# Chunk 0 of a delta-rule attention: U by 32-token blocks in the first half, step sizes in G's rows and x's diagonal, unread products between all stages, chunk 1's queries sooner

## The chip, the cores and the metric

The kernel runs on one core of a Trainium2 chip. The core has a matrix engine (PE, with its weight loads listed as PEld), a vector engine (DVE), an activation engine (ACT), a general engine (POOL) and a queue engine that issues most DMAs (SP). Each engine runs its instructions in order and waits on semaphores for the others. The metric is the device time of one execution in microseconds. The median of three runs of the kernel before is 638.62 us (637.84 to 638.83).

## The reference

Two things are computed, one after the other. First comes a linear attention with the delta rule, for 4 batches, 8 heads, 768 tokens and head dimension 48:

```python
k_n = k / (norm(k) + 1e-6)
state = zeros((B, H, D, D))
for t in range(S):
    kt, vt, bt = k_n[:, :, t], v[:, :, t], beta[:, :, t, None]
    y[:, :, t] = einsum('bhd,bhde->bhe', q[:, :, t], state)
    v_old = einsum('bhde,bhd->bhe', state, kt)
    state = state + bt * einsum('bhd,bhe->bhde', kt, vt - v_old)
```

Then a feed-forward layer over the 3072 tokens of 384 features that come out: `h = x @ w_in` (2048 wide), `g = h * sigmoid(h)`, `out = g @ w_out`. Weights arrive as 64-bit floats and are narrowed to 32 bits in the kernel.

## The kernel before, in words

**Chunks and halves.** The 768 tokens are cut into six chunks of 128, each into two halves of 64. Within a half, the recurrence becomes algebra: with A the scores of keys against later keys, the updates U of all tokens solve a triangular system whose inverse XI is built explicitly, and U is XI applied to v less what the state already holds. U (called z, tile `zbuf`) then gives the outputs (`first_outputs`, `new`) and the state's update (`update`). Batches go in two groups g (batches 0 and 1, batches 2 and 3). The two heads of a pair lie in opposite halves of the 128 partitions.

**The inverse of chunk 0.** `first_score` makes A on PE; `block_out` and `block_in` send its 32x32 diagonal blocks through DRAM, so that each of the 128 partitions holds one block as tile g, and x starts as the identity (`block_room`). `norm_steps` gets the key lengths on DVE, and `block_steps` the step size of every token (tile step). `invert_first` inverts the two 16x16 corners of all blocks on DVE: it scales g by step (L668), adds 15 rank-one updates (L676, L680), scales x by step (L683), and transposes x twice (L690, L694). PE, which has nothing to do meanwhile, runs unread products (`busy`, L347, 384 columns) so timed that some wait for steps 0, 1, 2, 4, 8 and 15, and the transposes of chunk 1's keys behind steps 10, 12, 14 and 15 (`turn`, L500).

**From corners to 64x64.** `joins(0)` then runs ten stages on PE, each for one group and each followed by copies on ACT and DVE: `corner` (L717, DVE L724) completes the 32x32 blocks, `turned` (L733) and `straight` (L746) give the 32x32 inverses in both orientations, and `merge_half` (L806), twice per group, gives the block that joins two 32-token blocks. Four `masks` on DVE (L1364) zero the query scores at and below the diagonal. `inner` (L840) multiplies the 64x64 inverse with v, `first_outputs` (L884) makes the outputs, and DVE's L893 completes their transposed form xT. From there the hidden layer (`hidden`, L1046) starts, into which a written text of letters (`script`) then weaves all further work of chunk 0's second half and chunk 1: r is one half of a hidden block, f a step of narrowing weights, j one product of `joins(1)`, q the transposes of one batch of chunk 1's queries, s a step of `solve`, b the start of a narrowing.

**Order.** `pin` ties every compute instruction behind the one before it on its engine, so the order in the program is the order on each engine. `in_line` does the same for SP's DMAs. The entries of `loads` are DMAs that are issued when a count of PE's instructions (4 for a product, 2 for a transpose) reaches a number. Narrowing a piece of weights takes two ACT instructions (L233, L234), two on DVE (L238, L242) and one on POOL (L246). PSUM has eight banks in three sets: A and CC, three each, and M, two, which the transposes of chunk 1 and the hidden layer use.

Of the kernel before, what the change touches and what calls it, by code (L numbers as in the profile page):

```python
# [19 lines left out]
def kernel(  # L20
# [322 lines left out]
    def busy(n=1, after=None, how=NoSync, wide=DM):  # L343

        for _ in range(n):
            pw = bank(CC, "pw")
            done = pin(nc.tensor.matmul(  # L347
                pw[:, 0:wide], lhsT=ident[:],
                rhs=states[0][:].rearrange("p u a w -> p (u a w)")[:, 0:wide], start=True, stop=True,
            ))  # L350
# [203 lines left out]
    def block_room(c):  # L554
# [10 lines left out]
        pin(nc.gpsimd.memset(x[:, 0 : T * T : T + 1], 1.0))  # L565
# [97 lines left out]
    def invert_first(step):  # L663
# [19 lines left out]
        yield pin(nc.vector.tensor_tensor(  # L683
            out=x2, in0=x2, in1=of.unsqueeze(3).to_broadcast([P, 2, Q, Q]), op=ALU.mult
        ))
# [55 lines left out]
        def straight(g, hf):  # L741
# [9 lines left out]
            for odd in (1, 0):  # L751
# [83 lines left out]
    def inner(c, g, hf, room=CC):  # L835

        pz = bank(room, "pz")
# [7 lines left out]
        if c == 0 and hf == 0:  # L845
            by = (by_act, by_dve) if g == 0 else (by_dve, by_act)
            at = slab[:, g * HB * NP * 2 * D + D :][:, 0 : HB * NP * 2 * D]
            by[0](at.rearrange("p (n w) -> p n w", w=2 * D)[:, :, 0:D], pz[:, 0:DM].rearrange("p (n d) -> p n d", d=D))
            by[1](to, by_heads(pz))
        else:  # L850
            by_act(to, by_heads(pz))
# [126 lines left out]
    def solve(c):  # L978

        if c == 0:  # L980
            together(inner(0, 0, 0, CC))
            together(inner(0, 1, 0, M))
            yield
            first_outputs(0)
            yield
# [334 lines left out]

    for b in range(2):
# [7 lines left out]
    first_queries(1)  # L1329
    step = block_steps(0)  # L1330
    for t in xis:
# [7 lines left out]
    busy(1)  # L1339
    for b in range(2, B):  # L1340
        turn(0, b, 1, M)
    for b in range(2, B):
# [4 lines left out]
        (WINDOW + PACKET * 3 + 90, fetch_w_in, 3),  # L1347
        (WINDOW + PACKET * 4 + 15, load_q, 1, slice(HB * 0, HB * 0 + HB)),
# [6 lines left out]
        (WINDOW + PACKET * 15 + 45, fetch_w_out, 3),  # L1355
        (WINDOW + PACKET * 15 + 60, fetch_w_out, 4),
# [5 lines left out]
    def masks(g, u):  # L1362
        to = aps[0, g][1][:, u]
        pin(nc.vector.tensor_tensor(  # L1364
            out=to, in0=to, in1=above[:].unsqueeze(1).to_broadcast([P, H, W]), op=ALU.mult
        ))

    for n in range(1 + Q):
        done = next(inv)
        if n in (0, 1, 2, 4, 8):  # L1370
# [13 lines left out]
    def joins(hf, between=()):  # L1384

        for stage in (
# [4 lines left out]
            for what in between[:1]:  # L1391
                what()
            between = between[1:]

    def filled(n):
        return lambda: fill(n)

    def sized():
        size_half(0, pins[seen_on])
        begin_next()  # L1400

    def none():
        pass

    together(joins(0, [
        lambda: (size_half(0, pins[seen_on]), begin_next(),),
        lambda: (),
        lambda: (),
        lambda: (fill(1), fill(1),),
        lambda: (fill(1),),  # L1410
        lambda: (),
        lambda: (fill(1),),
        lambda: (fill(1), begin_next(),),
        lambda: (),
        lambda: (),
    ]))
    masks(0, 0)
    masks(0, 1)
    masks(1, 0)
    masks(1, 1)  # L1420

# [217 lines left out]
```

## Time and profile before

| | before |
|---|---|
| median of three runs | 638.62 us (637.84 to 638.83) |
| the profiled execution, first to last instruction | 636.1 us |
| mean granted PE clock | 0.986 |
| PE busy | 622.4 us (98%) |
| DVE busy | 397.5 us (62%) |
| ACT busy | 214.3 us (34%) |
| POOL busy | 89.9 us (14%) |

The profiled execution has no time of its own beside its span of 636.1 us; the median of the runs is 2.5 us above that span. Times in rows are microseconds from the first instruction. A row of the timeline has start, duration, engine, line, operation, output and inputs, shapes and count, and in brackets how long the engine was idle before and what ended the wait. A product of 32-bit floats shows as two records, so x6 are three products. The ends of matmuls are modelled: each record's duration includes a tail that overlaps with the next one. "issue" in the chain of waits is time in which nothing that the profile shows was waited for. In rows of stretches the number behind the busy times is the granted clock of PE, 1.00 being full and 0.50 half.

### The profile page before, as it was taken

The page shows a single profiled execution, that of the slowest core. Times are in us where ns is not written, and L with a number is a line of the kernel's source. Part 1 is how long each engine was busy: PE and PEld are TensorE (multiplying, and loading weights), DVE is VectorE, ACT ScalarE, POOL GpSimd, SP SyncE. Part 2 cuts the span into 40 slices and gives each one's busy share as a digit, 9 for nine tenths or more (in the row PEclk, how much of TensorE's full clock was granted, in tenths as well). Part 3 has the DMA queues.
Part 4 walks back from the last instruction along what each step waited for, and adds up shares of the span by engine and source line. Part 5 has one row for each costly group of instructions (what it writes and reads, how often), then busy time and mean ns, then how long its engine had stood idle before and what let it go on. Part 6 is the DMA issues. An engine that isn't in the chain of part 4 may idle for free.

```text
span 636.1 us, 21387 instructions
## 1 busy us (share of the span) xinstructions
PE 622.4 (98%) x9406; PEld 547.3 (86%) x9406; DVE 397.5 (62%) x910; ACT 214.3 (34%) x500; POOL 89.9 (14%) x92
## 2 busy tenths in 40 slices
PE   7979999999999999999999999999999999999997
PEld 5568788656799989989989989989989989989997
DVE  5786879999677974546974555975455964112112
ACT  3456673423351122451122451122451122441120
POOL 5033721345020020020020010020002000000000
PEclk9779999999999999999999999999999999999999
DMA  7966726350458460459151359232253133010101
GB/s 114 227 159 177 218 67 148 100 99 4 95 105 174 72 104 8 94 107 183 37 91 21 75 124 164 56 84 29 64 117 76 26 75 37 16 38 1 26 0 26
DMA packets 145676, 54.70 MB, mean 86 GB/s; under 512 B 117152, under 2 KB 138912, under 8 KB 145584
## 3 DMA queue, kind: packets, MB, share of 16 engines
q1 hardware_dynamic: 143136, 52.93, 40.5%
q8 instruction: 74, 1.21, 0.8%
q10 hardware_dynamic: 2448, 0.41, 0.4%
q14 instruction: 18, 0.15, 0.1%
HBM read 40.14 MB, written 11.01 MB: 80 GB/s over the span
## 4 chain that ended last, share of the span: by engine, by line
PE 94%; DVE 2%; DMA 1%; issue 1%; ACTq 0%; ACT 0%; POOL 0%; SPq 0%; DVEq 0%; POOLq 0%
PE phid L1046 40%; PE px L1163 17%; PE py L1163 13%; PE po L1090 5%; PE pb_c L840 3%; PE pa L529 2%; PE pb_c L828 2%; PE pyc L919 2%; PE pb_c L1090 2%; PE pb_c L860 2%; PE pyc L906 1%; PE px L782 1%; PE py L782 1%; PE pt L500 1%; DMA sums_of_w<-blocks 1%
## 5 line engine op out<-in xcount | busy, mean ns | idle before, releaser
L1046 PE MATMUL phid<-xT,w_in 128*128 128x256 f32 x1152 | 257.0, 381 | 0.2 <-DVE xT L893 0.2
L1046 PEld LDWEIGHTS phid<-xT,w_in 128*128 128x128 f32 x1152 | 216.4, 190 | 30.2 <-issue 0.9
L1056 ACT ACTIVATE gT<-phid 128x512 f32<-128x512 f32 x88 | 52.5, 597 | 144.8 <-PE phid L1046 140.5
L1144 DVE TENSOR_TENSOR sums_of_g<-gT 128x384 f32<-128x384 f32 (+1 forms) x60 | 30.4, 529 | 65.7 <-ACT gT L1056 55.4
L627 DVE SCALAR_TENSOR_TENSOR rank<-g,step,x 128x31 f32<-128x31 f32 (+15 forms) x124 | 49.8, 401 | 21.7 <-DMA g<-blocks 18.1
L1163 PE MATMUL px<-sums_of_w,sums_of_g 128*128 128x192 f32 x320 | 56.6, 329 | 0.0
L1163 PE MATMUL py<-w_out,sums_of_g 128*128 128x192 f32 x320 | 56.2, 328 | 0.0
L1163 PEld LDWEIGHTS py<-w_out,sums_of_g 128*128 128x128 f32 x320 | 52.3, 190 | 0.3
L1163 PEld LDWEIGHTS px<-sums_of_w,sums_of_g 128*128 128x128 f32 x320 | 52.2, 190 | 0.4
L632 DVE TENSOR_TENSOR x<-x,rank 128x31 f32<-128x31 f32 (+15 forms) x124 | 42.5, 342 | 4.3
L467 POOL TENSOR_TENSOR vf<-vf,n_slot 128x768 f32<-128x768 f32 x10 | 14.8, 1494 | 174.4 <-DMA vf<-in_v_dram 150.4
L544 ACT COPY xT<-pyc 48x128 f32<-48x128 f32 (+2 forms) x126 | 32.7, 260 | 1.7
L488 DVE STREAM_TRANSPOSE kq<-stage 128x512 f32<-128x512 f32 x28 | 28.4, 1115 | 5.2 <-DMA stage<-in_q_dram 5.2
L1163 PE MATMUL py<-w_out,gT 128*128 128x192 f32 x160 | 28.9, 330 | 0.0
L1174 DVE TENSOR_TENSOR o<-o,kept 128x192 f32<-128x192 f32 (+1 forms) x29 | 11.5, 422 | 26.7 <-ACT kept L1171 26.7
L1163 PE MATMUL px<-w_out,gT 128*128 128x192 f32 x160 | 27.9, 327 | 0.0
L1163 PE MATMUL px<-sums_of_w,gT 128*128 128x192 f32 x160 | 27.8, 327 | 0.0
L1163 PEld LDWEIGHTS px<-w_out,gT 128*128 128x128 f32 x160 | 26.5, 190 | 0.6
L550 POOL COPY g<-x 64x256 f32<-64x256 f32 x4 | 5.0, 1242 | 151.9 <-DVE x L635 151.9
L1163 PEld LDWEIGHTS py<-w_out,gT 128*128 128x128 f32 x160 | 26.1, 190 | 0.4
L865 DVE TENSOR_TENSOR state<-state,pb_c 128x384 f32<-128x384 f32 x22 | 11.2, 550 | 24.1 <-PE pb_c L860 24.1
L1163 PEld LDWEIGHTS px<-sums_of_w,gT 128*128 128x128 f32 x160 | 26.2, 190 | 0.1
(222 smaller groups left out, 931.2 us busy)
## 6 DMA issues: line engine op xcount, KB each, us to landing
vf<-in_v_dram SPq DMA_DIRECT2D x48, 96.0 KB, 2.8
out_dram<-o SPq DMA_DIRECT2D x42, 96.0 KB, 2.2
w_out<-in_moe_w_in_dram SPq DMA_DIRECT2D x4, 768.0 KB, 4.7
sums_of_w<-in_moe_w_out_dram SPq DMA_DIRECT2D x4, 768.0 KB, 4.1
blocks<-ap SPq DMA_DIRECT2D x44, 64.0 KB, 1.9
g<-blocks SPq DMA_DIRECT2D x5, 512.0 KB, 3.5
kb<-in_k_dram SPq DMA_DIRECT2D x12, 192.0 KB, 4.2
kb<-in_k_dram SPq DMA_DIRECT2D x24, 96.0 KB, 4.3
```

The lines of the kernel that those rows point to most:

```text
L467: pin(nc.gpsimd.tensor_tensor(out=vf, in0=vf, in1=of, op=ALU.mult))
L488: pin(nc.vector.transpose(out=kqs[c, b][:, :, j, :].rearrange("p a (i m) -> p a m i", i=T), in_=src.rearrange("p a (m d) -> p a m d", d=D) ...
L529: pin(nc.tensor.matmul(pa[e][half, p * n * W : (p + 1) * n * W], lhsT=kq[rows, p, 0, half], rhs=kq[rows, p, js[0] : js[-1] + 1, half], sta ...
L544: return pin(nc.scalar.copy(to, of))
L627: pin(nc.vector.scalar_tensor_tensor(out=tv, in0=g[:, 0:m, m : m + 1].to_broadcast([P, m, n]), scalar=step[:, m : m + 1], in1=x[:, m : m + ...
L632: yield pin(nc.vector.tensor_tensor(out=x[:, 0:m, m:T], in0=x[:, 0:m, m:T], in1=tv, op=ALU.add))
L840: yield pin(nc.tensor.matmul(pz[rows, n * D : (n + 1) * D], lhsT=xis[g][rows, u * H + 2 * p + e, :], rhs=vfs[c][rows, hf, g * HB + u, p, : ...
L1046: pin(nc.tensor.matmul(ph[:, j * GT : (j + 1) * GT], lhsT=w_in[:, a, (2 * f + j) * P : (2 * f + j + 1) * P], rhs=xTs[c, hf][:, a, :], star ...
L1056: pin(nc.scalar.activation(out=hidden_of(c, hf, f), in_=ph[:], func=ACTF.Silu, scale=-0.5 if in_blocks(c) else 0.5))
L1090: pin(nc.tensor.matmul(pos[i][:, 0:DM], lhsT=hidden_of(0, hf, f // 2)[:, at : at + C], rhs=w_outs[f // HFF][:, f % HFF, :], start=(f == 0) ...
L1144: pin(nc.vector.tensor_tensor(out=sums_of_g[:, k, fs], in0=of[0], in1=of[1], op=op))
L1163: pin(nc.tensor.matmul(to, lhsT=at, rhs=quarter(f, *b) if isinstance(b, tuple) else sums_of_w[b][:, f], start=start and f == 0, stop=f == ...
```

## The change: what it does

- **Step sizes.** G's rows are scaled by the step sizes, not its columns; x starts with the step sizes on its diagonal (a POOL copy behind `block_steps`) and not with ones. The scaling of x behind the inversion (L683) goes.
- **U by blocks.** In the first half, `turned`, both `merge_half` and `inner` are gone. `first_block` makes U of the first 32 tokens, `across` takes what these contribute to the last 32 tokens' right side and DVE adds it to v, and `last_block` makes U of the last 32 tokens. ACT copies U to the slab for the outputs, and DVE copies it whole to z (`keep_last`).
- **Unread products.** A product of 512 columns in the banks M (`warm`) stands behind the second `corner`, behind each of the eight stages that follow and between the two `first_outputs`. During the inversion, one waits for every even step up to 14 and one stands behind the last transpose; one more is added ahead of the second pair's queries.
- **Order.** Group 0's masks move ahead of the inversion, group 1's behind the second `across`. v is scaled before the slab is cleared. Chunk 1's queries (first half) are loaded ahead of the fourth piece of w_in; two loads of w_out have lower counts. The text begins "s s f5 q j16 q j16" instead of "s f3 s q q s j32": the transposes of two batches of chunk 1's queries stand among the corners of the second half, and two more steps of narrowing stand behind the first outputs.

```diff
-        pin(nc.gpsimd.memset(x[:, 0 : T * T : T + 1], 1.0))
+        if c > 0:
+            pin(nc.gpsimd.memset(x[:, 0 : T * T : T + 1], 1.0))
...
-            out=g2, in0=g2, in1=of.unsqueeze(2).to_broadcast([P, 2, Q, Q]), op=ALU.mult
+            out=g2, in0=g2, in1=of.unsqueeze(3).to_broadcast([P, 2, Q, Q]), op=ALU.mult
...
-        yield pin(nc.vector.tensor_tensor(
-            out=x2, in0=x2, in1=of.unsqueeze(3).to_broadcast([P, 2, Q, Q]), op=ALU.mult
-        ))
...
-            for odd in (1, 0):
+            for odd in ((0, 1) if hf == 0 else (1, 0)):
...
+    def blocks_of(k):
+        return slice(W * k, W * k + T), slice(W * k + T, W * (k + 1))
+    both_blocks = {}
+    def first_block(g):
+        pz = both_blocks[g] = bank(CC, "pz")
+        for u, p, e, n, _, _ in of_heads():
+            even, _ = blocks_of(e ^ g)
+            yield pin(nc.tensor.matmul(
+                pz[even, n * D : (n + 1) * D], lhsT=xis[g][even, u * H + 2 * p + e, 0:T],
+                rhs=vfs[0][even, 0, g * HB + u, p, :], start=True, stop=True,
+            ))
+        for k, by in enumerate((by_act, (by_dve, by_act)[g])):
+            even, _ = blocks_of(k)
+            by(zbuf[even, g * HB : (g + 1) * HB, 0, :, 0:D], by_heads(pz)[even])
+    def across(g):
+        pr = bank(A, "pr")
+        for u, p, e, n, _, _ in of_heads():
+            even, odd = blocks_of(e ^ g)
+            yield pin(nc.tensor.matmul(
+                pr[odd, n * D : (n + 1) * D], lhsT=aps[0, g][0][even, u, 2 * p + e, T:W],
+                rhs=zbuf[even, g * HB + u, 0, p, 0:D], start=True, stop=True,
+            ))
+        for k in range(2):
+            _, odd = blocks_of(k)
+            to = vfs[0][odd, 0, g * HB : (g + 1) * HB]
+            pin(nc.vector.tensor_tensor(out=to, in0=to, in1=by_heads(pr)[odd], op=ALU.add))
+    def last_block(g):
+        pz = both_blocks[g]
+        for u, p, e, n, _, _ in of_heads():
+            even, odd = blocks_of(e ^ g)
+            yield pin(nc.tensor.matmul(
+                pz[odd, n * D : (n + 1) * D], lhsT=xis[g][odd, u * H + 2 * p + e, T:W],
+                rhs=vfs[0][odd, 0, g * HB + u, p, :], start=True, stop=True,
+            ))
+        at = slab[:, g * HB * NP * 2 * D + D :][:, 0 : HB * NP * 2 * D]
+        by_act(at.rearrange("p (n w) -> p n w", w=2 * D)[:, :, 0:D], pz[:, 0:DM].rearrange("p (n d) -> p n d", d=D))
...
+    masks(0, 0)
+    masks(0, 1)
     step = block_steps(0)
+    pin(nc.gpsimd.tensor_copy(
+        out=blocks[0][2].rearrange("p s t -> p (s t)")[:, 0 : T * T : T + 1], in_=step[:]
+    ))
...
-    busy(1)
+    busy(2)
...
-        (WINDOW + PACKET * 3 + 90, fetch_w_in, 3),
-        (WINDOW + PACKET * 4 + 15, load_q, 1, slice(HB * 0, HB * 0 + HB)),
+        (WINDOW + PACKET * 3 + 90, load_q, 1, slice(HB * 0, HB * 0 + HB)),
+        (WINDOW + PACKET * 4 + 15, fetch_w_in, 3),
...
-        (WINDOW + PACKET * 15 + 45, fetch_w_out, 3),
-        (WINDOW + PACKET * 15 + 60, fetch_w_out, 4),
+        (WINDOW + PACKET * 14 + 173, fetch_w_out, 3),
+        (WINDOW + PACKET * 14 + 188, fetch_w_out, 4),
...
-    for n in range(1 + Q):
+    for n in range(Q):
         done = next(inv)
-        if n in (0, 1, 2, 4, 8):
+        if n % 2 == 0 and n < Q - 1:
             busy(1, done, Sync)
...
         if n == 15:
-            busy(1, done, Sync)
             turn(1, 3, 0, M)
+            busy(1)
     corner, turned, straight = next(inv)
+    size_half(0, pins[seen_on])
     pin(nc.gpsimd.memset(slab, 0.0))
...
-    together(joins(0, [
-        lambda: (size_half(0, pins[seen_on]), begin_next(),),
...
-    ]))
-    masks(0, 0)
-    masks(0, 1)
-    masks(1, 0)
-    masks(1, 1)
+    def keep_last(g):
+        by_dve(zbuf[:, g * HB : (g + 1) * HB, 0, :, 0:D], by_heads(both_blocks.pop(g)))
+    def warm(n=1):
+        busy(n, wide=2 * GT, room=M)
+    for stage, then in (
+        (corner(0, 0), lambda: begin_next()),
+        (corner(1, 0), lambda: (fill(2), warm())),
+        (straight(0, 0), lambda: warm()),
+        (straight(1, 0), lambda: warm()),
+        (first_block(0), lambda: (fill(1), warm())),
+        (first_block(1), lambda: (begin_next(), warm())),
+        (across(0), lambda: warm()),
+        (across(1), lambda: (masks(1, 0), masks(1, 1), warm())),
+        (last_block(0), lambda: (keep_last(0), warm())),
+        (last_block(1), lambda: (keep_last(1), warm())),
+    ):
+        together(stage)
+        then()
...
-        "s f3 s q q s j32 b j20 r f j8 ...
+        "s s f5 q j16 q j16 b j20 r f j8 ...
```

In `solve(0)`, the two calls of `inner` go and a `warm` stands between the two `first_outputs`.

More of the change, by code (lines that the diff above doesn't have):

```diff
@@ L980, in solve @@
         if c == 0:
-            together(inner(0, 0, 0, CC))
-            together(inner(0, 1, 0, M))
-            yield
             first_outputs(0)
+            warm()
             yield
@@ L1319, in first_queries, with masks @@
         score(0, b, (1,), (A, CC), evacuate)
+    def masks(g, u):
+        to = aps[0, g][1][:, u]
+        pin(nc.vector.tensor_tensor(
+            out=to, in0=to, in1=above[:].unsqueeze(1).to_broadcast([P, H, W]), op=ALU.mult
+        ))
     for b in range(2):
```

45 lines of the change are left out of this document (8 added, 37 removed).

## The prediction

> **What bounds the kernel now.** I read the busy time and clock by stretches first, then the PE waits, then the chain of waits. Stretches: us from the start, length; busy us of PE, PEld, DVE, ACT, POOL with counts; granted clock; DMA share; GB/s.
>
> ```profile
> 33.63:38.45 4.82, 3.79 (x259) 3.33 (x259) 4.34 (x8) 2.65 (x5) 2.85 (x2) 1.00 0.46 86
> 38.45:48.69 10.24, 8.20 (x275) 8.00 (x279) 8.75 (x17) 4.86 (x11) 1.83 (x1) 0.50 0.63 185
> 48.69:52.46 3.77, 3.62 (x198) 3.23 (x191) 3.03 (x6) 3.10 (x7) 1.91 (x1) 1.00 0.55 109
> 52.46:636.20 583.74, 578.92 (x8346) 513.95 (x8346) 359.13 (x805) 190.32 (x448) 73.43 (x62) 1.00 0.39 79
> ```
>
> From 52.46 us, where the first product of the hidden layer starts, PE is busy for 578.92 of 583.74 us. All its waits behind that point:
>
> ```profile
> PE pyc L919 <- issue: 0.8, 1, 0.8
> PE pb_c L828 <- ACT ap L544: 0.4, 1, 0.4
> PE phid L1046 <- DVE xT L893: 0.2, 1, 0.2
> ```
>
> They add up to 1.4 us, so a microsecond won or lost before 52.46 arrives at the end. The change lies before it. The chain of waits there (start, us, what):
>
> ```profile
> 31.52 0.99 DVE sums_of_w L683
> ...
> 33.58 1.82 DVE sums_of_w L694
> ...
> 35.61 0.36 DVE sums_of_w L724
> ...
> 38.09 1.05 issue
> ...
> 41.62 1.35 issue
> ...
> 46.71 1.60 PE pz L840 x30
> ...
> 52.33 0.14 issue
> 52.46 1.53 PE phid L1046 x6
> ```
>
> DVE's inversion leads up to 35.40, then PE leads, with holes of 1.05 and 1.35 us, at half clock from 38.45 to 48.69. The question is when the changed kernel's PE reaches that first hidden product. The profile gives a span of 636.1 us and no time of its own beyond it; the median of the runs is 638.62, so I carry 2.5 us around the span unchanged.
>
> **The change, part by part.** *Step sizes.* L683 (0.99 us) goes; scaling G by rows is the same instruction as by columns. DVE's last transpose would end at 34.38 instead of 35.40. POOL now copies 32 step sizes into x's diagonal, behind ACT's copy of the steps; its nearest row is L691, and the first user is the first rank update:
>
> ```profile
> 18.82 0.19 ACT L450 COPY step<-pg 128x32 f32<-128x32 f32 x1 [0.33 <-PE pg L445]
> 22.06 0.69 DVE L668 TENSOR_TENSOR sums_of_w<-sums_of_w,step 128x512 f32<-128x512 f32 x1 [3.01 <-DMA sums_of_w<-blocks]
> 31.33 0.63 POOL L691 COPY sums_of_w<-pick 128x512 f32<-128x512 f32 x1 [18.33 <-DVE rank L676]
> 45.32 2.50 DVE L1364 TENSOR_TENSOR ap<-ap,above 128x512 f32<-128x512 f32 x4
> ```
>
> It can end at 19.64 and is needed at 22.75: zero (0.6 at most without this cover). The two clears of xi queue behind it and are needed only near 38. *Masks.* Two of four (0.63 each) move into DVE's 3.01 us wait for the blocks, the others behind the additions of the second group: zero. They hid nothing before either: 45.32 to 47.82 lay beside L840, which ran until 48.31. *POOL order*: v is scaled before the slab is cleared; about 1.5 us each, done by 37.4, needed after 39: zero. The additions (32x384) and block copies are at most a 128x384 copy, on DVE and on ACT:
>
> ```profile
> L547 DVE COPY z<-pb_c 128x384 f32<-128x384 f32 x1 | 0.6, 557 | 0.0
> ...
> L544 ACT COPY xT<-py 128x384 f32<-128x384 f32 x2 | 1.0, 481 | 0.2 <-PE py L884 0.2
> ```
>
> Two take 1.1 us at most, and between a group's stage and its user lie two unread products and the other group's stage (3.0, below): zero. Without that cover this would be up to 1.1 us at each of five hand-overs (rival A).
>
> *PE, up to the corners.* Step 14 of the inversion ends at 31.04 and the corners start at 33.63:
>
> ```profile
> 14.97 2.20 PE L347 MATMUL pb_c<-state,ident 128*128 128x384 f32 x6
> ...
> 30.82 0.22 DVE L680 TENSOR_TENSOR sums_of_w<-sums_of_w,rank 128x56 f32<-128x56 f32 x1
> ...
> 32.29 0.60 PE L500 MATMUL pt<-ident,kb 128*128 128x128 f32 x4
> 33.63 0.20 PE L717 MATMUL pl<-sums_of_w,ap 32*32 32x16 f32 x2 [0.74 <-DVE sums_of_w L690]
> ```
>
> A matmul is two records, so x6 are three unread products of 384 columns, 0.73 each. Now eight follow even steps, and one the last transpose. Step 12 ends some 1.1 us before step 14; its product and four transposes (0.60 less 0.16 of tail that overlaps) hold PE until about 31.25. Behind that stand step 14's product, two groups of four transposes and one more product: 31.25 + 0.75 + 0.88 + 0.75 gives 33.6, and I take 33.7 with the entries. So PE itself is late and the 1.02 us of DVE buys nothing: first loss.
>
> *Stages.* PE's busy time in five short stretches, each of one line: L717 (128 records, two corners), L733 (32 records, 32 columns, two blocks of the array in turn), L746 (64, four blocks), L884 (48) and L840 (64 at half clock):
>
> ```profile
> 33.50:35.30 1.80, 1.59 (x128) 1.43 (x128) 1.00 0.55 103
> 54.80:55.53 0.73, 0.68 (x32) 0.60 (x32) 1.00 0.67 255
> 57.30:58.23 0.93, 0.87 (x64) 0.76 (x64) 1.00 0.94 344
> 50.20:51.20 1.00, 0.93 (x48) 0.79 (x48) 1.00 0.94 186
> 44.70:48.50 3.80, 3.65 (x64) 3.49 (x64) 0.50 0.55 104
> ```
>
> Each has 0.19 of tail under which the next starts. Removed are turned, both merges and inner: 2 x 0.49 + 4 x 0.49 + 3.46 at half clock (some 1.8 at full). Added are six stages of 32 records with 48 columns over two blocks in turn; the nearest row is L733 with 32 columns, so 0.49 x 48/32 = 0.74 each (0.49 if columns did not matter). Hence 1.40 corners, 2 x 0.68 straight, 6 x 0.74, 2 x 0.74 first outputs: 8.7 us.
>
> *Unread products.* Ten, 128x512, one behind every stage but the last. The price:
>
> ```profile
> 63.20 0.22 PE L806 MATMUL pb_c<-xe_y,ap 32*32 32x32 f32 x2
> ...
> 64.85 0.21 PE L806 MATMUL py<-xe_y,ap 32*32 32x32 f32 x1
> ...
> 63.43 1.49 PE phid L1046 x6
> ...
> 76.19 4.08 PE phid L1046 x18
> ```
>
> Twelve more records of 256 columns add 2.59 us, 0.216 each; six alone, set between small products, take 1.61 (the last small start is 63.42 less the 0.19 us of one record, 63.23 or 63.24, the next 64.85). So 0.31 goes to entering and leaving the full array. One filler is 4 x 0.216 + 0.28 = 1.14; lower end 0.86 (no switching). Ten: 11.4 us. PE is in order and every filler stands ahead of the next stage. It covers the wait for ACT and DVE, but two fillers and the other group's stage exceed any such wait, so PE is never out of work and the chain is PE's sum. What is late next is PE itself, at every step.
>
> *Between first outputs and the hidden product* stand, as before, eight transposes in two groups and 52 corner products, now all of them beside the last xT copies. By rows: each group 0.44 and 0.28 of switching, the corners 104/128 x 1.40 = 1.1, together 2.5 us, more than the 1.4 that ACT and DVE need for xT. This wait of 0.14 goes.
>
> Sum: 33.7 + 8.7 + 11.4 + 2.5 = 56.3, against 52.46: **+3.8 us**. The first three rows tell why: between 33.63 and 52.46 PE was idle for 18.83 - 15.61 = 3.2 us, and 8.20 us of work at half clock cost 4.1 too much. These 7.3 us, and 0.2 of products saved, are what can be won; the fillers take 11.4. Lower end (fillers 0.86, stages 0.49): 33.7 + 7.2 + 8.6 + 2.5 = 52.0, -0.5.
>
> *Narrowing.* Steps before and up to the first hidden product stay eight, but two more stand behind xT:
>
> ```profile
> L238 DVE TENSOR_SCALAR w_in<-w_in 128x768 uint32<-128x768 uint32 x3 | 2.4, 810 | 0.1
> L242 DVE SCALAR_TENSOR_TENSOR w_in<-raw,w_in 128x768 uint32<-128x768 uint32 x2 | 1.9, 954 | 0.0
> ...
> 43.53 7.10 SPq L144 DMA_DIRECT2D sums_of_g<-in_q_dram  x6
> ...
> w_out<-in_moe_w_in_dram SPq DMA_DIRECT2D x4, 768.0 KB, 4.7
> ```
>
> DVE then has 0.81 + 0.95 + 0.81 ahead of the copies of chunk 0's second corners; the second of these comes some 0.4 us after PE asks for it (0 to 0.9, the latter if nothing else gives way): +0.4. *Loads.* The first half of chunk 1's queries is issued one place sooner on SP's queue (here 43.53), some three us earlier; the fourth piece of w_in goes behind it, issued near 44 and landed by 49 (4.7 us, last row), is read by ACT near 55: zero. The thresholds of two w_out pieces drop by the 32 products that are gone.
>
> Total +4.2: **642.8 us**, slower.
>
> **Rivals.** *A: the fillers only fill.* Were PE waiting for copies, they would cost nothing. Without them at full clock the copies lead: corners until 35.1; four L724 of 0.35 until 36.0; the second straight stage 0.7, its copies behind L238 and the first group's copies until 38.5; first block 0.74, tail 0.2 and two ACT copies 1.0; crossing 0.74, tail and two additions 1.3; last block 0.74, tail and slab copy 0.7; first outputs 0.74 and 2.5: 47.2, so 633.4, faster. Between 47.2 at nothing and 56.3 at 1.14, the turn lies near 0.66 us of path per filler; streaming alone is 0.86. Against it: x18 against x6. For it: holes of 1.05 and 1.35 exist today.
>
> *B: half clock stays in the inversion.* Before:
>
> ```profile
> 17.97:21.38 3.41, 2.52 (x14) 1.72 (x15) 1.00 (x8) 1.46 (x8) 0.00 (x0) 1.00 0.90 246
> 21.38:28.21 6.83, 6.83 (x76) 4.56 (x75) 5.43 (x20) 4.17 (x8) 0.00 (x0) 0.50 1.16 208
> ```
>
> A second product now fills a hole near 20.4, which may prevent the drop at 21.38 (my sum assumes so). If not, fillers take up to twice 0.65 us until the clock returns at 28.21, PE comes out one filler of 0.7 us behind and has no hole to catch up in: the corners start near 34.4, 643.5. [...]
>
> *C: the clock falls inside the chain* although filled; two periods of 3.41 us at half clock cost 3.4 more: 646.2. For it: two steps of the inversion take 1.2 us (14 from 22.75 to 31.04), of which a filler of 0.73 leaves PE idle two fifths. Against it: from 52.46 on, where full-array and small products alternate as they would in the chain, the clock is 1.00 throughout.
>
> *D: the lower prices hold*: 638.1, no change to be measured.
>
> **How the numbers follow.** The main case 0.42, B 0.25, C 0.11, D 0.09, A 0.13. 0.2% is 1.3 us, about what a measurement of this kernel tells from no change. Slower 0.78, same 0.09, faster 0.13. The range from D's 638.0 to short of C, 645.8, leaves out A and most of C.
>
> **What would show it.** Right: PE without a wait over 0.3 us from the corners on; ten pairs of 128x512 records, some 1.1 us from small product to small product; first hidden product near 56.3; clock 1.00 from 28.2 on. Step-size part right but worthless: DVE's transposes end near 34.4, with corners starting at 33.7 or later. Wrong: a first hidden product before 52.5, which needs stages under 0.5 us or fillers under 0.65.

## The result, and the profile after

The changed kernel takes 645.48 us (median of four runs, 644.29 to 646.46), the kernel before beside it 638.73 (637.84 to 639.07): a ratio of 1.010, 95% interval 1.0078 to 1.0121. That is 6.75 us slower, where 4.2 were forecast. The profiled execution, the slowest of the four, took 646.46 us with a span of 644.8, against the 636.1 of before.

The stretches of the changed kernel (us from the start, length; busy us of PE, PEld, DVE, ACT, POOL with counts; granted clock; DMA share; GB/s):

```profile
17.97:21.38 3.41, 2.94 (x16) 2.15 (x17) 2.19 (x10) 1.46 (x8) 2.25 (x3) 1.00 0.85 248
21.38:28.20 6.82, 5.86 (x80) 2.94 (x77) 5.70 (x20) 3.96 (x8) 0.70 (x1) 1.00 1.28 204
33.19:55.64 22.45, 22.44 (x677) 13.74 (x676) 14.23 (x24) 9.62 (x19) 4.67 (x3) 1.00 0.48 122
55.64:251.92 196.28, 194.23 (x3013) 158.44 (x3007) 158.30 (x340) 77.11 (x156) 53.25 (x40) 1.00 0.46 109
253.80:257.21 3.41, 3.41 (x27) 3.34 (x14) 3.12 (x6) 1.15 (x2) 0.00 (x0) 0.50 0.02 5
257.21:644.75 387.54, 383.68 (x5309) 353.64 (x5308) 199.71 (x462) 112.57 (x290) 22.06 (x23) 1.00 0.34 64
```

The corners start at 33.19, the first hidden product at 55.64. Between them PE is busy for 22.44 of 22.45 us at full clock, where before it had 3.2 us of holes and 10.24 us at half clock. So the chain became what the change says, dense and at full clock, and is still 3.18 us later at its end (55.64 against 52.46). The fifth row is new: a half clock of 3.41 us in a place that the change doesn't touch.

What the chain consists of, from the chain of waits of the changed kernel (start, us, what), and below it the group of the unread products (busy, mean ns of one record):

```profile
35.90 0.15 PE pl L744 x2
...
36.61 1.05 PE pw L347 x2
...
39.49 0.80 PE pb_c L856 x32
40.29 1.05 PE pw L347 x2
41.34 0.80 PE pb_c L856 x32
```

```profile
L347 PE MATMUL pw<-state,ident 128*128 128x512 f32 x20 | 11.3, 644 | 0.0
L856 PE MATMUL pb_c<-vf,xi 32*32 32x48 f32 x64 | 1.7, 202 | 0.0
```

An unread product takes 1.05 us of path, a block stage 0.80, one behind the other without a gap. The waits of PE behind the corners in the changed kernel, with the two rows of the timeline in which the larger ones end:

```profile
PE px L780 <- issue: 1.6, 1, 1.6
PE phid L1081 <- issue: 1.0, 1, 1.0
PE pyc L943 <- issue: 0.4, 1, 0.4
PE pb_c L826 <- ACT ap L544: 0.4, 1, 0.4
PE pyc L956 <- issue: 0.4, 1, 0.4
```

```profile
92.00 1.24 PE L1081 MATMUL phid<-xT,w_in 128*128 128x256 f32 x5 [0.96 <-issue]
253.57 0.18 PE L780 MATMUL px<-crossed,y 32*32 32x32 f32 x1 [1.64 <-issue]
```

They add up to 3.8 us, where before 1.4 stood behind the first hidden product. Matched product by product, the changed kernel lies 3.18 us behind at the first hidden product, 2.2 at 90.5, 3.3 at 92.0, 4.7 at 173, 7.8 at 274 and 8.7 at 562. So 5.4 of the 8.6 us in the two profiled spans arise behind the chain: 2.4 are the difference of the waits, about 1.7 the half clock behind the largest one, the rest I could not place in single rows. All these waits but one are "issue", with nothing in the profile that ends them, and they interrupt a stage in its middle.

**What these waits have in common.** I numbered all records of TensorE in order (products, weight loads, and the semaphore and drain instructions between them), and set beside each wait the transfers of the instruction queue, of which the page has one line, the same for both kernels: 74 packets, 1.21 MB, so 16,384 bytes each.

```profile
q8 instruction: 74, 1.21, 0.8%
```

Worked out from the traces:

```
kernel   wait          us    number of the record   last packet starts   PE goes on after
before   38.09-39.14   1.05   1218 = 4*256 + 194     36.72                2.42 us
before   41.62-42.97   1.35   1473 = 5*256 + 193     40.78                2.19
before   86.88-87.65   0.77   4034 = 15*256 + 194    85.33                2.32
after    91.04-92.00   0.96   4033 = 15*256 + 193    89.54                2.46
after   160.07-160.51  0.44   5570 = 21*256 + 194   158.13                2.38
after   251.92-253.57  1.64   8129 = 31*256 + 193   251.13                2.43
after   455.03-455.39  0.37  14530 = 56*256 + 194   452.75                2.64
```

The changed kernel has 9370 products and 9370 weight loads by the page and 148 of the other records in its trace, 18,888 in all, and 18,888/256 is 73.8. In the fourteen executions profiled for this document there are 80 "issue" waits of 0.3 us or more behind the corners' start. 74 of them lie at a number of 193 or 194 modulo 256, and all 74 end 2.17 to 3.21 us after a packet of 16,384 bytes started. The other six lie elsewhere: four are at the first product of `turned`, which starts 0.1 us behind DVE's copy of the corners (experiment 4 has the rows), two wait for a copy on ACT (experiment 6). Read the other way round, it is the same: in none of the 1024 crossings of such a number in these traces does TensorE pass it less than 2.17 us after the packet that stands in the same place in the order started, and no packet starts while TensorE is more than 44 records short of the crossing before.

My reading of these counts is that a packet holds the code of 256 records, 64 bytes each (16,384/256), that one packet is ahead at a time, and that PE stops where the next one hasn't come. The profile names nothing that ends these waits, so this is inferred from the numbers; "wait for code" and "packet boundary" below mean a wait at such a number and the number itself. Measured are the numbers, the 2.17 to 3.21 us from the start of a packet to PE's going on, and, where PE stops at one packet after another, 3.83 us between the ends of the stops (39.14 and 42.97 before). Two corners are 256 records that start within 1.4 us (33.63 to 35.03 before), while no two packets of the two kernels' profiled executions start less than 3.28 us apart.

So two theories: the new waits behind the chain come with the *position* of the packets in the work (**code theory**: the change removes 72 records ahead of the first hidden product, so every packet behind it ends at another place), or with the change's own *edits*, its loads, masks and unread products. And within the chain: do the unread products cost their full price, or do they only fill time in which PE would wait for copies or code?

### The profile page after: what moved, and what is told of

Same layout as the page of the kernel before. It is cut to its first block, busy times and chain, and to the rows that moved or that the text cites. A ratio compares the mean times of both kernels' runs of the same rounds, so it can differ in the third digit from the quotient of the medians.

```text
span 644.8 us, 21310 instructions
## 1 busy us (share of the span) xinstructions
PE 631.9 (98%) x9370; PEld 547.4 (85%) x9370; DVE 398.8 (62%) x908; ACT 213.4 (33%) x497; POOL 90.9 (14%) x92
## 3 DMA queue, kind: packets, MB, share of 16 engines
q8 instruction: 74, 1.21, 0.8%
## 4 chain that ended last, share of the span: by engine, by line
PE 94%; DMA 1%; DVE 1%; issue 1%; ACT 1%; SPq 1%; POOL 0%; ACTq 0%; DVEq 0%; POOLq 0%
PE phid L1081 39%; PE px L1198 17%; PE py L1198 12%; PE po L1125 5%; PE pb_c L838 2%; PE pa L529 2%; PE pb_c L826 2%; PE pyc L956 2%; PE pw L347 2%; PE pb_c L1125 2%; PE pb_c L897 1%; PE pyc L943 1%; PE pt L500 1%; PE pb_c L347 1%; PE px L780 1%; PE py L780 1%
## 5 line engine op out<-in xcount | busy, mean ns | idle before, releaser
L1198 PE MATMUL px<-sums_of_w,sums_of_g 128*128 128x192 f32 x320 | 58.2, 335 | 0.0
L1198 PEld LDWEIGHTS px<-sums_of_w,sums_of_g 128*128 128x128 f32 x320 | 53.8, 195 | 0.4
L1209 DVE TENSOR_TENSOR o<-o,kept 128x192 f32<-128x192 f32 (+1 forms) x29 | 11.4, 419 | 27.0 <-ACT kept L1206 27.0
```

Of the source, the lines that this page charges most:

```text
L1198: pin(nc.tensor.matmul(to, lhsT=at, rhs=quarter(f, *b) if isinstance(b, tuple) else sums_of_w[b][:, f], start=start and f == 0, stop=f == ...
```

## The experiments

All keep the computation; added products are unread. Four kernels ran beside each other in each of three groups; the kernel before had medians of 640.40, 639.77 and 639.61 us there.

**1. The 72 records back.**

```diff
     block_in(0)
     busy(1)
+    pad(18)        # 18 unread products of 32x32x32: 72 records
```

> The changed kernel with 18 unread products of 32x32x32 (72 PE instructions: two weight loads and two matmuls each) in PE's wait near 13.4 us, which has room for about 1 us; they bring PE's instruction number at the first hidden product back to that of the kernel before. Code theory (PE's code arrives in packets of 256 instructions, every wait that the profile calls issue lies at an instruction number that leaves 193 or 194 over 256 and ends 2.2 to 2.5 us after the start of the last packet, and the change moved the bursts of small products against these numbers): the waits of 0.96, 0.44, 1.64 and 0.37 us near 91, 160, 252 and 455 us go, the one of 0.77 near 90 returns, and behind the first hidden product the distance to the kernel before stays near +3.2 us, so about 638.7 + 3.2 = 641.9 us. Order theory (the narrowing, loads and copies that were moved come too late for PE further on): the waits stay where they are, 645 us or more.

645.61 us (644.55 to 647.74), ratio 1.0076 (1.0059 to 1.0093). The waits at 92, 160, 252 and 455 are gone, as the code theory says, and others at packet boundaries stand at 87.3 (0.30 us), 90.2 (1.38) and 360.2 (0.77); but the time isn't won, because PE now waits for a late move of xT, and 3.4 us at half clock follow:

```profile
101.36 1.01 PE L1081 MATMUL phid<-xT,w_in 128*128 128x256 f32 x2 [2.11 <-DMA xT<-part]
```

Half of the theory stands; this wait needed a run of its own (experiment 10). I had overlooked that the kernel places its later loads by TensorE's instruction count: with 18 products more, each load came 72 records of work sooner.

**2. Ten unread products of 32 columns**, as many instructions, a sixteenth of the work; **3. of 256 columns.**

```diff
-        busy(n, wide=2 * GT, room=M)
+        busy(n, wide=32, room=M)      # experiment 2
+        busy(n, wide=GT, room=M)      # experiment 3
```

> The changed kernel with the ten unread products between the stages 32 columns wide instead of 512: the same number of PE instructions, so the same packets of code. Price theory (each 512-wide product costs PE 1.14 us on the path): 10 x 0.8 us of streaming go, but waits for copies, for code and a half clock can come back in the chain; first hidden product between 48 and 53 us instead of 55.6, 637.5 to 642.5 us. Rival (the wide products only fill waits and hold the clock): first hidden product at 55 us or later, clock 0.50 for some 10 us, no faster than 645 us. Code theory: behind the first hidden product the waits near 91, 160, 252 and 455 us stay, some 5 us.

> The changed kernel with these ten products 256 columns wide. Price theory: 10 x 0.43 us less, first hidden product near 51.4 us, clock 1.00 in the chain, 641.2 us; if the clock falls within the chain, up to 3.4 us more. Rival (waits are what is filled): first hidden product stays near 55.6 us, 645.5 us.

With 32 columns: 649.98 us (648.92 to 652.28), ratio 1.0155 (1.0132 to 1.0178). First the clock from 38.78 to 55.85 with 32 and with 256 columns, then the waits in the chain with 32, then with 256:

```profile
38.78:55.85 17.07, 16.69 (x315) 15.18 (x316) 7.54 (x13) 5.48 (x11) 1.84 (x1) 0.50 0.42 113
```

```profile
38.78:55.85 17.07, 16.30 (x451) 12.19 (x451) 11.36 (x21) 8.77 (x15) 3.43 (x2) 1.00 0.60 155
```

```profile
35.33 0.17 PE L715 MATMUL pb_c<-sums_of_w,ap 32*32 32x16 f32 x1 [0.95 <-issue]
...
39.16 0.25 PE L744 MATMUL pl<-sums_of_w 32*32 32x32 f32 x1 [1.60 <-issue]
```

```profile
35.73 0.17 PE L715 MATMUL pb_c<-sums_of_w,ap 32*32 32x16 f32 x1 [1.29 <-issue]
...
39.55 0.21 PE L744 MATMUL pl<-sums_of_w 32*32 32x32 f32 x1 [1.02 <-issue]
```

With 32 columns the chain stands at half clock for 17.07 us and waits for code, and the first hidden product comes at 58.01: the unread products held the clock (1.00 with 256 columns in this stretch, 0.50 with 32), and without their work this chain is longer, not shorter. In time and clock that is the outcome written down for the rival; as the clock fell, it says nothing of the products' price at full clock, and experiment 3 has to. With 256 columns the median is 643.93 us (ratio 1.0063, 1.0032 to 1.0095; single runs from 642.92 to 654.83, where the three above 650 have a mean clock of 0.976 to 0.984 and the others 0.997 to 1.00). The chain takes 20.59 instead of 22.45 us, 1.86 less, although 2.31 us of code waits have come in: the products alone gave back 4.17, and 20 records of 256 columns at 0.216 are 4.3. The price per record was right, and more than half of what narrower products save is lost at packet boundaries. The waits end 3.83 and 3.82 us apart, as before.

**4. The step sizes alone**, in the kernel before.

```diff
-            out=g2, in0=g2, in1=of.unsqueeze(2)...
+            out=g2, in0=g2, in1=of.unsqueeze(3)...
...
-        yield pin(nc.vector.tensor_tensor(
-            out=x2, in0=x2, in1=of.unsqueeze(3)..., op=ALU.mult
-        ))
```

> The kernel before with the step sizes in G's rows and x's diagonal alone, without the scaling of x (0.99 us on DVE). PE there waited 0.74 us for DVE's transposes ahead of the corners. If the gain reaches PE: corners 0.7 us earlier, 637.7 to 638.1 us. If the waits for code further on take it back (their place in the stream is the same, the packets come 0.7 us earlier too): they don't, by the code theory. Rival (POOL's strided copy or the later clears of xi delay something): 638.7 us or more.

640.51 us (638.43 to 641.06), ratio 0.9998 (0.9986 to 1.0010): no difference. Where the microsecond went shows against a profile of the unchanged kernel on that chip (experiment 0, below). First the unchanged kernel, then the step sizes alone:

```profile
35.19 0.21 PE L733 MATMUL pl<-sums_of_w 32*32 32x32 f32 x2 [0.62 <-issue]
...
39.21 0.26 PE L806 MATMUL pb_c<-xe_y,ap 32*32 32x32 f32 x1 [1.43 <-issue]
...
43.04 0.21 PE L806 MATMUL pb_c<-xi,xe_y 32*32 32x32 f32 x1 [1.35 <-issue]
```

```profile
34.11 0.21 PE L731 MATMUL pl<-sums_of_w 32*32 32x32 f32 x2 [0.41 <-issue]
35.78 0.21 PE L731 MATMUL pb_c<-sums_of_w 32*32 32x32 f32 x1 [1.12 <-issue]
...
39.79 0.26 PE L804 MATMUL pb_c<-xe_y,ap 32*32 32x32 f32 x1 [2.16 <-issue]
...
43.62 0.20 PE L804 MATMUL pb_c<-xi,xe_y 32*32 32x32 f32 x1 [1.36 <-issue]
```

The first row of each is the first product of `turned`, which waits for DVE's copy of the corners; of the unchanged kernel, a copy that ends at 35.09, 0.10 us before the product starts:

```profile
34.79 0.30 DVE L724 SCALAR_TENSOR_TENSOR sums_of_w<-pl,second,pick 64x128 f32<-64x128 f32 x1
```

The other rows lie at packet boundaries. The corners start at 32.30 instead of 33.16, 0.86 sooner, and the waits for code in the chain grow from 2.78 to 4.64 us; the last two of them end no sooner although DVE is done sooner, at 39.79 and 43.62 against 39.21 and 43.04.

**0. The kernel before, for its profile on that chip.**

> The kernel before, unchanged, for its profile beside the other three of this group. Both theories expect it at 640.4 us, the median that it had beside the first four experiments, or at the 638.7 of the first group; the first hidden product at 52.5 to 53.5 us, and TensorE's waits that nothing in the profile ends at the same instruction counts as before (956, 1218, 1473 and 4034 of weight loads and matmuls together).

One run, 641.28 us; first hidden product at 53.39, waits at 956, 1218, 1473 and 4034 as expected.

**5. The kernel before with its packets where the changed kernel has them.** It gets 184 records more, which is 72 fewer modulo 256; none of the change's edits. **8.** The same with the loads kept at their places in the work.

```diff
     block_in(0)
     busy(1)
+    pad(46)        # 46 unread products of 32x32x32; experiment 8: not counted for the loads
```

> The kernel before with 46 unread 32x32x32 products in an early idle stretch of TensorE: 184 instructions more, which is 72 fewer modulo 256, so that behind the first hidden product its instructions stand to the 256-instruction packets as those of the changed kernel do. Code theory: packets end about 3.8 us apart when they are asked for back to back, so the waits move: in the chain the boundaries now fall 78, 334 and 590 instructions behind its start and the first hidden product comes 1.4 us later than in the kernel before, at about 54; behind it the waits of the changed kernel appear in a kernel that has none of its edits (near 90 about 1 us, 159 about 0.4, 250 about 1.6 us with a stretch of half clock behind it): 644 to 647 us in all. Rival, that these waits come from the changed kernel's moved loads, masks and unread products: nothing behind the first hidden product changes against the kernel before, 640 to 642 us.

> As the kernel before with 46 tiny products, but these aren't counted where the planned loads are placed by TensorE's instruction count: in the earlier run every load behind them was issued 184 instructions of work too soon, here each load keeps its place in the work and only the packet boundaries move. Code theory: the waits of the changed kernel (near 92 about 0.9 us, 158 to 162 about 0.6 together, 253 about 1.65 with 3.4 us at half clock behind it) stay, 645 to 648 us. Rival, that they came from the earlier loads: they go, 641 to 643 us.

647.40 us (645.45 to 647.82), ratio 1.0111 (1.0083 to 1.0138), and with the loads kept 648.95 (645.69 to 651.27), 1.0145 (1.0108 to 1.0182). Both lie a little above what I expected. The kernel before, with 46 unread little products, is as slow as the changed kernel or slower. Of experiment 5, then of experiment 8, the wait that the changed kernel has at 253.57, and the stretch behind it:

```profile
255.18 0.18 PE L782 MATMUL px<-crossed,y 32*32 32x32 f32 x1 [1.66 <-issue]
```

```profile
256.14:259.55 3.41, 3.41 (x13) 3.41 (x12) 3.10 (x7) 0.61 (x2) 0.00 (x0) 0.50 0.02 5
```

```profile
256.12 0.26 PE L782 MATMUL px<-crossed,y 32*32 32x32 f32 x1 [1.70 <-issue]
```

```profile
255.43:262.26 6.83, 6.13 (x46) 5.64 (x49) 3.90 (x8) 1.30 (x3) 0.00 (x0) 0.50 0.01 2
```

The same product, the same length (1.64, 1.66, 1.70), the half clock behind it: for this wait the rival, that it comes from the edits or the moved loads, falls. The smaller ones came in part: 0.84 us at 93.6 and 0.36 at 162.1 in experiment 5, 0.49 at 94.9 in experiment 8. The chain has other waits too: its waits for code are 1.56, 2.63 and 0.71 us in experiment 5 and 1.04, 4.29, 0.98 and 1.72 in experiment 8, and the first hidden product comes at 57.43 and 58.90, 4.0 and 5.5 later than the unchanged kernel's 53.39, where I expected 1.4. Two things beside the packets have a share in that. The 46 products take 3.09 us (13.47 to 16.56) where PE had 0.98 us to spare, and the corners start at 34.31 and 34.52, against 33.63 and 33.16 in the two profiles of the unchanged kernel; and the half clock in the chain lasts 17.06 and 13.66 us, against 10.24 and 13.65. For the wait of 4.29 us the packet started 3.55 us after the wait before it had ended, later than elsewhere; why isn't shown.

**6. The kernel before with 8 such products**, meant to have the next packet start sooner; **9.** the same with the loads kept; **7.** 8 products in the variant with 256 columns.

```diff
     block_in(0)
     busy(1)
+    pad(8)
```

> The kernel before with 8 such products, 32 instructions: the packet boundary that now lies 6 instructions behind the start of the corners (705 against 699) is then passed some microseconds ahead of them, while TensorE waits for VectorE, and the next packet is asked for that much sooner. Code theory: the waits of 0.46 and 0.13 us at 35.2 to 36.0 go, the one at 38.1 shrinks by some 0.4, the one at 41.6 too, the first hidden product comes 0.3 to 0.6 us sooner (about 52.0 where the kernel before has 52.5), and the end moves by that, and by waits behind it that may shift by some tenths either way: ratio 0.998 to 1.000. Rival, that those holes are waits for the corners' copies: they stay, ratio 1.000 to 1.001.

> As the kernel before with 8 tiny products, the loads kept at their places in the work. Theory of the loads: the wait for the moves of xT at 99 to 100 (1.18 us, not in the kernel before) is the price of w_out's loads, issued 32 instructions sooner and so ahead of it in the DMA engines: it goes, and with it 1 to 1.5 us: 645 to 646. Code theory: the waits at packet boundaries inside the chain (0.76, 1.09, 1.30, 1.15) and at 86 to 91, 352 and 439 stay within some tenths, as the instruction counts are the same. Rival, that the whole of the 7 us came from the loads: back to 640 to 641.5.

> The changed kernel with 256 columns in each of the ten unread products, and 8 tiny products early as in the run of the kernel before with 8: the boundary at 705 is passed ahead of the corners (they start at 734 instead of 702). Code theory: the hole of 1.29 us behind the first corner goes, the one of 1.02 in the straight stages shrinks or moves, the first hidden product at 52.5 to 53.2 instead of 53.67; behind it the waits at 89 and 250 move with the 32 instructions and stay about as large together (2 to 3.5 us): 642 to 644 us. Rival, that narrower products cost this much because the stages wait for their copies: first hidden product stays at 53.5 to 53.8, 643.9 us.

The number of the records moved and the waits did not go: 647.06 us (645.99 to 647.93), ratio 1.0113 (1.0090 to 1.0136), and with the loads kept 644.99 (643.69 to 647.73), 1.0080 (1.0056 to 1.0104). The eight products take 0.69 us and fit into PE's 0.98 us of idle time, so here the cost isn't their own work. The packet that I wanted sooner started at 32.3 us in experiment 6, near the unchanged kernel's 32.1, though TensorE stood 33 records further, at record 730 instead of 697; with 18 products it started at 25.58, with TensorE at 729. In records these two agree, and TensorE merely came to 730 late, as it waits for DVE there; but in experiments 4 and 5 the same packet started at 826 and 827. What decides when a packet starts I could not settle, so the position's price can't be worked out ahead. In both, PE waits 1.15 us for ACT's copy of xi, which stands behind two conversions of weights; of experiment 9, PE and then ACT:

```profile
46.65 0.43 PE L840 MATMUL pb_c<-vf,xi 64*64 64x48 f32 x3 [1.15 <-issue]
```

```profile
45.20 0.96 ACT L234 ACTIVATE w_out<-w_out,plus 128x768 int32<-128x768 uint32 x1
46.19 0.62 ACT L544 COPY xi<-px 32x256 f32<-32x256 f32 x2
```

The wait for xT's move is there with the loads moved (1.18) and kept (1.06), so the moved loads aren't its cause. The runs of experiment 7 lie between 642.53 and 657.79 and nothing rests on their median of 650.32; the profiled one, the longest, stood at half clock from 37.7 to 61.6, so products of 256 columns held the clock in some executions (1.00 from 38.78 to 55.85 in experiment 3) and not in others.

**10. The 72 records back, the loads kept**; **11.** 144 records, the loads kept.

```diff
     block_in(0)
     busy(1)
+    pad(18)        # experiment 11: pad(36); neither counted for the loads
```

> The changed kernel with 18 tiny products, so that its packets lie behind the first hidden product as the kernel before has them, and now the loads at the changed kernel's own places in the work. Theory of the loads: the wait of 2.11 us for the moves of xT at 99 to 101, and the 3.4 us of half clock that followed it, go: first hidden product 55.2, then only waits at packet boundaries (87 to 91.5 about 1.7, 262 and 360 and 456 about 1.1 together): 641.5 to 643 us, still 1 to 2.5 above the kernel before, of which 2.7 are the longer chain. Rival, that the late move belongs to the change itself: it stays, 645 to 646.

> The changed kernel with 36 tiny products, 144 instructions, loads at the changed kernel's own places: another position of the packets, for the spread that the position alone gives. Code theory: first hidden product between 55 and 57, behind it waits at other places, the one at 252 gone or elsewhere, 641 to 647 us. Were the position without effect, it would be 645.5 as without these products.

Experiment 10: 645.19 us (644.15 to 647.75), ratio 1.0096 (1.0067 to 1.0125). The late move of xT stays, 2.00 us, and with it the half clock, so my theory of the loads falls again. Part of its cause is in ACT's rows; of the changed kernel, then of experiment 10 with the waits of PE:

```profile
90.23 0.58 ACT L544 COPY part<-pyc 48x512 f32<-48x512 f32 x1 [1.11 <-PE pyc L956]
```

```profile
91.62 0.58 ACT L544 COPY part<-pyc 48x512 f32<-48x512 f32 x1 [2.50 <-PE pyc L956]
```

```profile
91.37 0.27 PE L956 MATMUL pyc<-ap,z 64*64 64x64 f32 x2 [1.11 <-issue]
...
101.06 1.10 PE L1081 MATMUL phid<-xT,w_in 128*128 128x256 f32 x4 [2.00 <-DMA xT<-part]
```

In experiment 10 a packet ends three records short of the end of L956, whose result ACT must copy before xT can be moved: the copy is 1.39 us later (91.62 against 90.23), the moves are issued from 94.5 on instead of 93.1, and PE waits for them. That is not all: the last of the five moves is issued at 97.2 against 96.6, only some 0.6 us later, but takes 3.7 us to land, where none of the changed kernel takes more than 2.9, as far as the profile tells the landings. Of the five moves, in the changed kernel and in experiment 10:

```profile
DMA to landing us min/median/max: 2.0/2.4/2.9
```

```profile
DMA to landing us min/median/max: 1.8/2.1/3.7
```

Why that move lands so slowly no run shows. In the changed kernel the packet ends a little behind L956, among the hidden layer's products, where only PE itself loses the time. So the place of a wait seems to count as much as its length. The unchanged kernel has its wait at 89.07 inside that stage too (0.94 us) without a late move behind it; why there the moves come in time I didn't follow.

Experiment 11: 658.31 us (656.92 to 665.74), ratio 1.0319 (1.0259 to 1.0378), far above the 641 to 647 that I expected: 18.7 us above the kernel before beside it, where the changed kernel lay 6.75 above, so some 12 us for 36 products that take 2.46 us themselves. Its two largest waits, each with 3.41 us of half clock behind it:

```profile
354.25 0.23 PE L780 MATMUL px<-crossed,y 32*32 32x32 f32 x2 [2.32 <-issue]
...
448.37 0.55 PE L826 MATMUL pb_c<-state,kq 48*64 48x48 f32 x19 [1.97 <-issue]
```

Side by side, with the position of the packets behind the chain counted from the kernel before (records modulo 256); the third column adds the "issue" waits of at least 0.3 us at packet boundaries behind the corners' start:

| kernel | position | first hidden product, us | waits, us | time, us |
|---|---|---|---|---|
| before (two profiles) | 0 | 52.46, 53.39 | 3.2, 3.7 | 638.7 to 640.4 |
| before, 8 products (6; 9) | 32 | 54.73; 55.21 | 7.6; 7.1 | 647.06; 644.99 |
| before, 46 products (5; 8) | 184 | 57.43; 58.90 | 7.8; 11.3 | 647.40; 648.95 |
| after | 184 | 55.64 | 3.4 | 645.48 |
| after, 18 products (1; 10) | 0 | 55.17; 55.62 | 2.2; 1.1 | 645.61; 645.19 |
| after, 36 products (11) | 72 | 57.36 | 9.6 | 658.31 |

At position 0 the changed kernel is some 5.6 us slower than the kernel before (645.19 against 639.61). At position 184 each has to be set against the kernel before of its own group: the changed kernel lies 6.75 us above it, the kernel before with 46 products 7.63 and 9.34, and the intervals of the three ratios overlap. So "slower" holds against the kernel before as it stands, and isn't shown at every position. Position and added products together move the kernel before by 5 to 9 us and the changed one by up to 12; with 46 and 36 products the two aren't separated, with eight, which fit into an idle stretch, the position is what is left. What the edits are worth at the best position of each is open: four positions of 64 were tried, and none of these kernels beats the kernel before.

## Why the prediction was right or wrong

**The sum was right for the chain.** The first hidden product was put at 56.3 and came at 55.64. By terms: corners' start 33.7, measured 33.19; ten unread products 11.4, measured 10.5 (1.05 each, so the 0.28 for switching was 0.19); stages 8.7, measured 9.6 (corners 1.66 for 1.40, straight stages 0.71 and 0.76 for 0.68, blocks 0.80 and first outputs 0.86 for 0.74); 2.5 between first outputs and hidden product, measured 2.3. In the chain PE had no wait and the clock was 1.00, as "What would show it" asked. Behind the chain these two signs failed: waits of 0.37 to 1.64 us, and half clock from 253.80.

**The step sizes bought nothing, for the reason given and for one more.** DVE's transposes end at 34.11 (forecast 34.38, before 35.40):

```profile
32.16 1.95 DVE L692 STREAM_TRANSPOSE sums_of_w<-sums_of_w 128x1024 f32<-128x1024 f32 x1
```

PE was not out of work until 33.19. Experiment 4 shows that the saving is lost without the unread products as well, to longer waits at packet boundaries (4.64 us against 2.78).

**"A microsecond won or lost before 52.46 arrives at the end" is the step that failed.** I took the 1.4 us of waits behind that point for a constant. One of them, the 0.77 at 87.65, was a wait for code, and it moved with the 72 removed records; waits of 0.96, 0.44, 1.64 and 0.37 us and 3.41 us at half clock came at other places, and 3.2 us at the chain's end became 8.6 at the kernel's. Experiments 5 and 8 show the largest of these waits, and some of the others, in a kernel with none of the edits. The forecast's 4.2 lay 2.5 below the measured 6.75, for this reason.

**That the total came near is in part luck.** The chain cost 3.18 where 3.8 were forecast, the 0.4 for narrowing wasn't there, and 5.4 us that the prediction put at nothing came in behind it: in the two profiled spans more than the chain itself. The 645.48 lies 0.3 us inside the upper end of the range, 645.8. The sign, too, held for the kernel before with its own packets; with 46 more products it is as slow as the changed one.

**The term for narrowing (+0.4) was not seen**: PE has no wait ahead of the second corners.

**Rival A** was refuted as a mechanism by experiment 3: from its corners' start the chain took 22.45 us with 512 columns and 20.59 with 256, at full clock and in spite of 2.31 us of new waits for code, so the products cost their price. (With 32 columns it took 24.99, but at half clock.) What I gave for it, "holes of 1.05 and 1.35 exist today", was a misreading: these are the waits at records 1218 and 1473, for code by my reading and not for copies. By that reading they can be filled, but only with work that brings no instructions: 1449 records from 699 to 2148 are 5.7 packets, and at 3.83 us a packet, one of them ahead, an estimate from these rows gives 17.8 us for a chain that took 18.83. By this estimate there was about one microsecond to win there (2.7 at 3.47 us a packet, the shortest distance seen), not the seven that I counted in holes and half clock.

**Rival B** didn't happen: the clock stayed at 1.00 from 17.97 to 28.20, in the first two rows of the result. With one more product in the stretch from 17.97 to 21.38 (PE busy for 2.94 us of 3.41, where before it was 2.52) the clock held, in the changed kernel and in five of its six variants (experiment 11 has 3.41 us at half clock from 16.41), so the chance of 0.25 was probably too high. **Rival C** is nearest in its number, 646.2, and not in its mechanism: the clock fell, once, 200 us behind the chain. **Rival D** was refuted by the products' 1.05 and the blocks' 0.80.

## What to carry to other kernels

When a wait ends in nothing that the profile shows and cuts a stage of small products in its middle, number the engine's records. Here 74 of 80 such waits lay at 193 or 194 modulo 256; I read them as waits for code, and 72 records more took four of them away (at 92, 160, 252 and 455, experiment 1) and brought others. Where small products stood alone, 256 records took about 3.8 us from stop to stop, and what was saved on DVE was lost there (experiment 4); wide products, few instructions for much work, paced it and held the clock (ten of 512 columns: 22.45 us at 1.00). Before a per-cent difference is put down to an edit, run the old kernel with as many unread products as bring its records to the same position: here 46 of them made the old kernel as slow as the changed one. Check that they fit into an idle stretch; the eight did, the 46 did not.

## What was not expected of the hardware

- Eight to 46 unread products of 32x32x32 early in the program cost 5 to 9 us in the kernel before, 36 of them some 12 in the changed one; by themselves they take 0.69 to 3.09 us.
- A wait for code of 1.64 to 2.32 us at times came with 3.41 or 6.83 us at half clock (253.80, 256.14, 255.43, and behind both waits of experiment 11), of which half, 1.7 or 3.4 us, is lost by my estimate.
- The ends of waits for consecutive packets lay 3.83 us apart in most kernels (3.82 to 3.83 in the chain of experiments 2, 3 and the unchanged kernel), but 3.47 to 5.92 elsewhere. A packet started when TensorE stood anywhere from 44 records short of the boundary before to 255 past it; what decides within that wasn't settled.
